# Output weights in runs of four rows, hidden units taken with a step of four, and two more loads of the second batch held behind a weight

## The chip, the cores and the metric

The kernel runs on one core of a Trainium2 chip. The metric is the device time of one execution in microseconds (us), lower is better. One execution was also taken by the hardware profiler; where a number below comes from its page or its trace, the time runs from the start of the profiled span.

## What is computed

The reference is an attention with 16 extra "beacon" keys, followed by a gated feed-forward network (FFN) over the same tokens:

```
B, H, S, Nb, D = 8, 8, 576, 16, 64
k_all = concat([beacon_k, k]);  v_all = concat([beacon_v, v])       # 592 keys for each head
scores = q @ k_all.T / 8, causal over the 576 own keys, beacons seen by all
a = softmax(scores);  x = a @ v_all                                  # 4608 tokens x 512
out = (relu(x @ w_gate) * (x @ w_val)) @ w_out                       # 512 -> 1536 -> 512
```

Inputs and output are float32 in memory. The order of the 1536 hidden units is free: any permutation gives the same output, if the columns of `w_gate` and `w_val` and the rows of `w_out` are permuted alike.

## The kernel before

Matrix work is done in bf16 with float32 sums. The kernel works batch by batch on the attention and span by span on the FFN: the spans are 240 and 336 tokens (together batch 0), then 512 each, and 448 at the end.

**Attention.** `new_batch` loads the inputs of a batch through staging tiles `st` (8 of them, `N_ST`): first two "rest" loads K and Q, then for each pair of heads a k load and a q load, and five v loads. The order of a batch after the first is the string `"KQ0011v2233vvvv"` (line 648), where 0 0 1 1 are k and q of head pairs 0 and 1, here called k0, q0, k1, q1 of batch 1. All these loads are issued by the SP engine, in one queue, in the planned order. GpSimd (POOL) or VectorE rounds a staged tile to bf16 (line 511, called the cast here), TensorE (PE) transposes it (line 522). Scores are line 740, the softmax is VectorE line 688, ScalarE line 695 and POOL line 706, the product with v is line 836.

**FFN.** `ffn(m0, mt, ...)` does, for each of 12 blocks of 128 hidden units, four matmuls on `wg_r` (line 897), ReLU on ScalarE (908), four matmuls on `wv_r` (902), the product on VectorE (913); then, for each 128 tokens, 12 matmuls on `wo_r` (928), an eviction to an `osb` tile (line 460 on ScalarE, 462 on VectorE) and a store (942). The weight operand of lines 897 and 902 (the part loaded into the array by LDWEIGHTS) is a contiguous slice of 128 columns. Only the very last piece of 64 tokens is done in two halves of 256 columns: both halves land in one `osb` tile, on partitions 0 to 63 and 64 to 127, the first half is stored by SP, the second by the queue of ScalarE.

**Weights.** Nine transfers, all issued by POOL (line 474), with a cast from float32 to bf16 on the way: gate and value in three column blocks each (512 columns, called g0, v0, g512, v512, g1024, v1024), and `w_out` in three blocks of four times 128 rows (wo0, wo4, wo8). Each of the nine consists of 512 runs of 512 values, 2 KB in memory and 1 KB in SBUF.

**The order of work** is written by a planner (`Plan.order`): every piece of work is a task with engines, a cost and a priority, and a list schedule with these costs fixes the order of the instructions of each engine. On the chip each engine goes through its own list in order, and waits only for data and buffers. A load can therefore be issued earlier than the planner thought, as soon as its staging tile is free. `HELD` is the means against it: `HELD[(b, at)]` gives the load at place `at` of batch `b` a marker on POOL (a memset of one element of its staging tile, line 532), which is planned behind the issue of the named weight; the load is behind the marker, and so are the batch's later loads. Before, only K of batch 1 is held, behind v0. While PE has nothing to do, the planner puts filler matmuls (line 987) into its list.

Of the kernel before, what the change touches and what calls it, by code (L numbers as in the profile page):

```python
# [34 lines left out]
PEQ = lambda b, g: b < 1  # L35
ENG = [("POOL", "DVE"), ("POOL",), ("POOL",)]
F_MOST = 3
HELD = {(1, 0): ("v", 0, 0)}
BEHIND = {(2, 7): (1, 1)}
MARK = 0.08  # L40
AB_FIRST = 0
# [4 lines left out]
OUT = -1300.0  # L46
ORDER0 = ("k00", "q00", "K", "Q", "k10", "q10", "v", "v", "k01", "q01", "k11", "q11", "v", "v", "v")
W_COLS = [(0, 512), (512, 512), (1024, 512)]
W_ROWS = 4
W0 = 9.0  # L50
W_STEP = 3.4
W_ISSUE = 0.85
# [114 lines left out]
class Plan:  # L167
# [7 lines left out]
    def add(self, engines, cost, run, deps=(), holds=(), prio=0.0, lag=None, part=0, lazy=0.0, after=0.0, move=0.0):  # L175
        t = Task(engines if isinstance(engines, tuple) else (engines,), cost, run, deps, holds, prio, lag, part, lazy, move)
        t.ready = after
        for d in t.deps:
            d.users.append(t)
        self.tasks.append(t)  # L180
        return t
# [108 lines left out]
def kernel(  # L290
# [12 lines left out]
    nc = tc.nc  # L303
# [5 lines left out]
    P = 128  # L309
# [29 lines left out]
    def many(n, shape, dtype, name):  # L339
        return [cp.tile(shape, dtype, name=f"{name}{i}") for i in range(n)]  # L340
# [4 lines left out]
    xT = cp.tile([P, KM, NT], BF16, name="xT")  # L345
    sel = xT[:, KM - 1, NT - 2 * P:].bitcast(FP32).rearrange("p (g j) -> p g j", j=TAIL)
    wg_r = cp.tile([P, KM, DFF], BF16, name="wg_r")
    wv_r = cp.tile([P, KM, DFF], BF16, name="wv_r")
# [14 lines left out]
    osb_s = Slots(many(N_OSB, [P, DM], FP32, "osb"))  # L363
# [10 lines left out]
    f_s, v_ps, first_ps = Share(banks, F_MOST), Share(banks, V_MOST), Share(banks, FIRST_MOST)  # L374
# [3 lines left out]
    add = plan.add  # L378


    def c_dve(n):
        return 0.07 + 0.00104 * n
# [7 lines left out]
    def c_act(n):  # L390
        return 0.06 + 0.00083 * n
# [4 lines left out]
    def c_pe(n):  # L396
        return 0.003 + n / 2400.0
# [60 lines left out]
    def copy(e, dst, src):  # L458
        if e == "ACT":
            nc.scalar.copy(dst, src)  # L460
        elif e == "DVE":
            nc.vector.tensor_copy(dst, src)  # L462
        else:
            nc.gpsimd.tensor_scalar(dst, src, 1.0, 1.0, ALU.mult, ALU.mult)  # L464
# [1 line left out]

    wg_s = moe_w_gate.rearrange("(ko ki) n -> ki ko n", ki=P)
    wv_s = moe_w_val.rearrange("(ko ki) n -> ki ko n", ki=P)
    wo_s = moe_w_out.rearrange("(ko ki) n -> ki ko n", ki=P)
    weight_in = {}  # L470

    def weight(kind, ko, kos, n0, w, prio, work):
        d, s = {"g": (wg_r, wg_s), "v": (wv_r, wv_s), "o": (wo_r, wo_s)}[kind]
        x = add("POOL", W_ISSUE, lambda t: nc.gpsimd.dma_start(
            d[:, ko:ko + kos, n0:n0 + w], s[:, ko:ko + kos, n0:n0 + w]), (), (), work, 0.1, move=0.78 * kos * w / 512,
            after=W0 + W_STEP * len(weight_in) / KM)
        for i in range(kos):
            for c in range(n0, n0 + w, 512):
                weight_in[kind, ko + i, c] = x
# [10 lines left out]
    def new_batch(b, prio, work):  # L490
# [35 lines left out]
        def staged():  # L526
            nonlocal held
            st = Hold(stage_s, 2)
            after = HELD.get((b, at)) or BEHIND.get((b, at))
            if after:  # L530
                st.users += 1
                held = add("POOL", MARK, lambda _: nc.gpsimd.memset(st.tile[:1, :1], 0.0), (), (st,), work - 30)
                if (b, at) in HELD:
                    weight_in[after].soon.append(held)
# [351 lines left out]
            one(what)  # L886


    def ffn(m0, mt, deps, prio):
        hid, vals = [], []  # L890
        hT = [Hold(hid_s, 1 + (mt + P - 1) // P) for _ in range(NF)]
        for nf in range(NF):
            psg, psv, g = Hold(f_s, 2), Hold(f_s, 2), Hold(gate_s, 2)

            def gate(_, nf=nf, psg=psg):
                for ki in range(KM):
                    nc.tensor.matmul(psg.tile[:, :mt], wg_r[:, ki, nf * P:(nf + 1) * P], xT[:, ki, m0:m0 + mt],  # L897
                                     start=(ki == 0), stop=(ki == KM - 1))

            def val(_, nf=nf, psv=psv):  # L900
                for ki in range(KM):
                    nc.tensor.matmul(psv.tile[:, :mt], wv_r[:, ki, nf * P:(nf + 1) * P], xT[:, ki, m0:m0 + mt],  # L902
                                     start=(ki == 0), stop=(ki == KM - 1))

            n0 = nf * P // 512 * 512
            a = add("PE", 4 * c_pe(mt), gate, deps + vals[max(nf - 3, 0):max(nf - 2, 0)] + [weight_in["g", ki, n0] for ki in range(KM)], (psg,),
                    prio + 0.02 * nf)
            r = add("ACT", c_act(mt), lambda _, psg=psg, g=g: nc.scalar.activation(  # L908
                g.tile[:, :mt], psg.tile[:, :mt], AF.Relu), (a,), (psg, g), -1000 + prio)
            b_ = add("PE", 4 * c_pe(mt), val, [a] + [weight_in["v", ki, n0] for ki in range(KM)], (psv,),  # L910
                     prio + 0.02 * nf + 0.01)
            vals.append(b_)
            hid.append(add("DVE", c_dve(mt), lambda _, psv=psv, g=g, nf=nf: nc.vector.tensor_mul(  # L913
                hT[nf].tile[:, :mt], g.tile[:, :mt], psv.tile[:, :mt]), (r, b_), (psv, g, hT[nf]), -1000 + prio))
        prev = None
        for t0 in range(0, mt, P):
            rows = min(P, mt - t0)

            halves = 2 if rows <= 64 else 1
            w = DM // halves  # L920
            ps, osb = Hold(f_s, 4 if halves == 1 else 3), Hold(osb_s, 2 * halves)
            prev = prev if halves > 1 else None
            k = NF // 3 * (2 * halves - 1)
            for part in range(NF // k):
                def outp(_, part=part, t0=t0, rows=rows, ps=ps, w=w, halves=halves, k=k):
                    for nf in range(k * part, k * part + k):
                        for c in range(halves):
                            nc.tensor.matmul(ps.tile[64 * c:64 * c + rows, :w], hT[nf].tile[:, t0:t0 + rows],  # L928
                                             wo_r[:, nf, w * c:w * c + w], start=(nf == 0), stop=(nf == NF - 1))

                need = [prev] + hid[k * part:k * part + k] + [weight_in["o", nf, 0] for nf in range(k * part, k * part + k)]
                if part == 0:
                    need += hid[:11]
                prev = add("PE", k * c_pe(w) + SWITCH * (halves - 1), outp, need, (ps,) + tuple(hT[k * part:k * part + k]),
                           prio + 0.3 + 0.01 * part - (0.5 if part else 0))
            for c in range(halves):
                def evict(x, c=c, ps=ps, osb=osb, rows=rows, w=w):
                    copy(x.engine, osb.tile[64 * c:64 * c + rows, :w], ps.tile[64 * c:64 * c + rows, :w])

                def store(_, c=c, osb=osb, rows=rows, t0=t0, w=w):  # L940
                    q_ = nc.scalar if c else nc.sync
                    q_.dma_start(out[m0 + t0:m0 + t0 + rows, w * c:w * c + w], osb.tile[64 * c:64 * c + rows, :w])

                ev = add("ACT" if c else ("ACT", "DVE"), {"ACT": c_act(w), "DVE": c_dve(w)}, evict, (prev,), (ps, osb), -1000 + prio)
                add("DMA", (0.4, 0.78 / halves), store, (ev,), (osb,), prio + OUT)


    T0 = 10.0
# [1 line left out]
    for n0, w in W_COLS:  # L950
        for kind in "gv":
            weight(kind, 0, KM, n0, w, -15 + 0.3 * i, WWORK + 0.01 * i - (50 if i < W_FIRST else 0))
            i += 1
    for ko in range(0, NF, W_ROWS):
        weight("o", ko, W_ROWS, 0, DM, -15 + 0.3 * i, WWORK + 0.01 * i - (50 if i < W_FIRST else 0))
        i += 1
# [20 lines left out]
    for i, (m0, mt) in enumerate(spans):  # L977
        deps = []
        for b in range(B):
            for what, lo, hi in (("AB", 0, G0), ("CDE", G0, G0 + G1), ("F", S - TAIL, S)):  # L980
                if b * S + lo < m0 + mt and b * S + hi > m0:
                    deps += [x_done[b, what, p] for p in range(NP if what != "F" else 1)]
        ffn(m0, mt, deps, 1000 + 10.0 * i)
# [37 lines left out]
```

## Time and profile before

| what | value |
|---|---|
| median of 3 runs | 407.6 us (406.13 to 408.1) |
| the profiled execution, whole | 406.64 us |
| its span on the core | 404.8 us |
| PE busy | 393.2 us, 97% |
| LDWEIGHTS busy | 206.6 us, 51% |
| VectorE, ScalarE, POOL busy | 293.5, 259.7, 233.4 us |
| TensorE clock granted | full (1.00) |
| DMA | 67.99 MB in 174147 packets, mean 168 GB/s |

The span is what lies between the first and the last instruction on the core; 1.84 us of the execution lie around it. A matmul's duration in the profile is longer than the distance to the next one, since matmuls are pipelined: a group of eight 512-column matmuls takes about 0.216 us for each further one. POOL issues the nine weight transfers at 15.7, 18.2, 23.0, 26.0, 29.8, 32.8, 45.2, 56.6 and 59.5 us. Queue q0 carries them, queue q1 all loads and stores of SP.

### The profile page before, as it was taken

How to read it: one execution, taken by the hardware profiler on the slowest of the kernel's cores; microseconds unless marked ns; L12 is line 12 of the kernel's file. 1: busy time of each engine (PE TensorE's matmuls, PEld its weight loads, DVE VectorE, ACT ScalarE, POOL GpSimd, SP SyncE). 2: the span in 40 equal slices, each digit the busy share in tenths (PEclk: the TensorE clock that was granted, in tenths of full speed). 3: DMA queues.
4: the chain of work that ended last, by engine and by line, in shares of the span. 5: the costliest groups of instructions: out<-in, count | busy, mean ns of one | idle time of the engine just before them, and what ended most of it. 6: DMA issues, size and time to landing. Idle time of an engine off the chain costs nothing.

```text
span 404.8 us, 9993 instructions
## 1 busy us (share of the span) xinstructions
PE 393.2 (97%) x3320; PEld 206.6 (51%) x3320; DVE 293.5 (73%) x1051; ACT 259.7 (64%) x809; POOL 233.4 (58%) x450
## 2 busy tenths in 40 slices
PE   7998999999999999999999999999999999999995
PEld 4666864655445545544454545454444454444543
DVE  4997799887877897777898988698777733442432
ACT  2988688857696896758695778588757721330320
POOL 6897769947495977576787778577564420000000
PEclk9999999999999999999999999999999999999999
DMA  7999897998998999979899999699848273001102
GB/s 182 216 222 214 182 219 143 198 181 235 191 230 185 238 181 255 197 175 192 227 194 203 249 233 176 164 306 212 154 78 175 42 145 125 0 0 53 52 2 91
DMA packets 174147, 67.99 MB, mean 168 GB/s; under 512 B 146384, under 2 KB 169552, under 8 KB 174096
## 3 DMA queue, kind: packets, MB, share of 16 engines
q1 hardware_dynamic: 169264, 62.57, 72.5%
q0 software_dynamic: 4752, 4.72, 7.3%
q8 instruction: 26, 0.43, 0.5%
q14 instruction: 25, 0.20, 0.2%
q10 hardware_dynamic: 80, 0.07, 0.1%
HBM read 38.54 MB, written 9.44 MB: 119 GB/s over the span
## 4 chain that ended last, share of the span: by engine, by line
PE 88%; POOL 5%; DMA 4%; DVE 1%; issue 1%; SPq 0%; ACT 0%; POOLq 0%
PE f L928 24%; PE f L902 23%; PE f L897 23%; PE f L740 7%; PE f L836 6%; PE f L522 4%; DMA wv_r<-in_moe_w_val_dram 3%; POOL xT L706 2%; PE f L859 1%; PE f L987 1%; POOL pb L706 1%; DMA st<-in_beacon_k_dram 1%; POOL v L464 1%; PE f L790 1%; DVE f L688 1%
## 5 line engine op out<-in xcount | busy, mean ns | idle before, releaser
L706 POOL TENSOR_SCALAR pb<-pb,small 128x320 bf16<-128x320 bf16 (+8 forms) x272 | 141.5, 538 | 80.7 <-DVE small L701 75.8
L695 ACT ACTIVATE pb<-f,small 128x320 bf16<-128x320 f32 (+8 forms) x272 | 144.5, 555 | 23.5 <-DVE small L688 14.0
L688 DVE CUSTOM_DVE_ANT_0 f<-f,mask 128x320 f32<-128x320 f32 (+8 forms) x288 | 134.3, 516 | 11.7 <-PE f L740 8.1
L897 PE MATMUL f<-xT,wg_r 128*128 128x512 bf16 (+3 forms) x480 | 106.2, 358 | 1.7 <-DMA wg_r<-in_moe_w_gate_dram 1.6
L902 PE MATMUL f<-xT,wv_r 128*128 128x512 bf16 (+3 forms) x480 | 107.0, 358 | 0.7 <-DMA wv_r<-in_moe_w_val_dram 0.7
L908 ACT ACTIVATE g<-f 128x512 f32<-128x512 f32 (+3 forms) x120 | 66.8, 567 | 62.3 <-PE f L897 58.1
L913 DVE TENSOR_TENSOR hT<-g,f 128x512 bf16<-128x512 f32 (+3 forms) x120 | 75.1, 632 | 38.5 <-PE f L902 35.1
L928 PE MATMUL f<-wo_r,hT 128*128 128x512 bf16 (+2 forms) x456 | 101.3, 374 | 0.0
L897 PEld LDWEIGHTS <-wg_r 128*128 128x128 bf16 x480 | 45.2, 98 | 45.0 <-DMA wg_r<-in_moe_w_gate_dram 1.8
L902 PEld LDWEIGHTS <-wv_r 128*128 128x128 bf16 x480 | 44.2, 98 | 43.4 <-issue 2.3
L928 PEld LDWEIGHTS <-hT 128*128 128x128 bf16 (+2 forms) x456 | 41.9, 100 | 47.6 <-issue 3.4
L695 ACT ACTIVATION_READ_ACCUMULATOR pb<-f,small 128x1 f32 x272 | 61.0, 224 | 0.0
L511 POOL TENSOR_SCALAR h<-st 128x512 bf16<-128x512 f32 (+1 forms) x92 | 48.4, 541 | 7.8 <-DMA st<-in_k_dram 2.2
L688 DVE DVE_READ_ACCUMULATOR2_ANT small<- 128x1 f32 x296 | 42.3, 143 | 0.2 <-issue 0.2
L740 PE MATMUL f<-kT,qT 64*64 64x64 bf16 (+7 forms) x640 | 35.5, 292 | 1.0 <-ACT pb L695 1.0
L462 DVE COPY osb<-f 128x512 f32<-128x512 f32 (+2 forms) x26 | 17.7, 681 | 23.8 <-PE f L928 23.7
L701 DVE RECIPROCAL small<-small 128x2 f32<-128x2 f32 (+3 forms) x144 | 22.1, 162 | 14.2 <-ACT pb L695 9.2
L522 PE MATMUL f<-ident,h 128*128 128x128 bf16 (+1 forms) x320 | 27.8, 219 | 1.1 <-POOL h L511 0.8
L522 PEld LDWEIGHTS <-h 128*128 128x128 bf16 (+1 forms) x320 | 20.9, 99 | 14.0 <-POOL h L511 3.5
L740 PEld LDWEIGHTS <-qT 64*64 64x64 bf16 x640 | 15.0, 105 | 23.8 <-issue 18.4
L836 PE MATMUL f<-pTb,v 128*64 128x320 bf16 (+3 forms) x488 | 26.0, 253 | 0.0
L836 PEld LDWEIGHTS <-v 128*64 128x64 bf16 (+1 forms) x512 | 20.6, 109 | 9.7 <-issue 7.2
(60 smaller groups left out, 235.3 us busy)
## 6 DMA issues: line engine op xcount, KB each, us to landing
out_dram<-osb SPq DMA_DIRECT2D x34, 256.0 KB, 2.3
st<-in_k_dram SPq DMA_DIRECT2D x32, 256.0 KB, 4.3
st<-in_q_dram SPq DMA_DIRECT2D x32, 256.0 KB, 4.8
st<-in_v_dram SPq DMA_DIRECT2D x24, 256.0 KB, 5.7
st<-in_v_dram SPq DMA_DIRECT2D x8, 224.0 KB, 5.3
wg_r<-in_moe_w_gate_dram POOLq DMA_DIRECT2D x3, 512.0 KB, 11.1
wv_r<-in_moe_w_val_dram POOLq DMA_DIRECT2D x3, 512.0 KB, 11.6
wo_r<-in_moe_w_out_dram POOLq DMA_DIRECT2D x3, 512.0 KB, 6.4
```

What stands on the lines that cost most here:

```text
L511: (nc.gpsimd if x.engine == "POOL" else nc.vector).tensor_scalar(to, src, by, 1.0, ALU.mult, ALU.mult)
L522: nc.tensor.matmul(to, h16.tile[:rows, a * P:(a + 1) * P], ident[:rows, :rows], start=True, stop=True)
L688: nc.vector.tensor_tensor_reduce(out=view(i, n - m), in0=view(i, n - m), in1=msk, scale=1.0, scalar=at(7) if m < n else 3.0e38, op0=ALU.ad ...
L695: nc.scalar.activation(ph.tile.rearrange("p a n -> p (a n)")[:, a:a + n], view(i), AF.Exp, bias=at(i), scale=-1.0, accum_out=at(4 + i))
L706: nc.gpsimd.tensor_scalar(one, one, at(8 + i), 1.0, ALU.mult, ALU.mult)
L740: nc.tensor.matmul(banks[k][b_].tile[64 * i:64 * i + 64, off:off + n], t.q.tile[r, 2 * g + i, 64 * j:64 * j + 64], t.kT.tile[r, 2 * g + i, ...
L836: nc.tensor.matmul(ps.tile[64 * hh:64 * hh + 64, d0:d0 + w], t.v.tile[:rows, c, D * h:D * h + D], rhs(64 * hh), start=(c == 0), stop=(c == ...
L897: nc.tensor.matmul(psg.tile[:, :mt], wg_r[:, ki, nf * P:(nf + 1) * P], xT[:, ki, m0:m0 + mt], start=(ki == 0), stop=(ki == KM - 1))
L902: nc.tensor.matmul(psv.tile[:, :mt], wv_r[:, ki, nf * P:(nf + 1) * P], xT[:, ki, m0:m0 + mt], start=(ki == 0), stop=(ki == KM - 1))
L908: r = add("ACT", c_act(mt), lambda _, psg=psg, g=g: nc.scalar.activation(g.tile[:, :mt], psg.tile[:, :mt], AF.Relu), (a,), (psg, g), -1000 ...
L913: hid.append(add("DVE", c_dve(mt), lambda _, psv=psv, g=g, nf=nf: nc.vector.tensor_mul(hT[nf].tile[:, :mt], g.tile[:, :mt], psv.tile[:, :m ...
L928: nc.tensor.matmul(ps.tile[64 * c:64 * c + rows, :w], hT[nf].tile[:, t0:t0 + rows], wo_r[:, nf, w * c:w * c + w], start=(nf == 0), stop=(n ...
```

## The change

Three things are changed together. `w_out` is read so that each partition gets four consecutive rows in one run of 8 KB; the hidden units of a block of 512 are thereby dealt out with a step of four, and the 128 columns that lines 897 and 902 take from `wg_r` and `wv_r` are every fourth one. Two more loads of batch 1 are held: k0 behind the issue of g1024, k1 behind the issue of v1024 (the loads between and after them follow in SP's queue). And each half of the last 64 tokens gets an `osb` tile of its own.

```diff
-HELD = {(1, 0): ("v", 0, 0)}
+HELD = {(1, 0): ("v", 0, 0), (1, 2): ("g", 0, 1024), (1, 4): ("v", 0, 1024)}
...
-    wo_s = moe_w_out.rearrange("(ko ki) n -> ki ko n", ki=P)
+    wo_s = moe_w_out.rearrange("(c ki ko) n -> ki c ko n", ki=P, ko=W_ROWS)
...
-        x = add("POOL", W_ISSUE, lambda t: nc.gpsimd.dma_start(
-            d[:, ko:ko + kos, n0:n0 + w], s[:, ko:ko + kos, n0:n0 + w]), (), (), work, 0.1, move=0.78 * kos * w / 512,
+        src = s[:, ko // W_ROWS] if kind == "o" else s[:, ko:ko + kos, n0:n0 + w]
+        x = add("POOL", W_ISSUE, lambda t: nc.gpsimd.dma_start(d[:, ko:ko + kos, n0:n0 + w], src), (), (), work, 0.1, move=0.78 * kos * w / 512,
...
+    def units(nf):
+        return nf // W_ROWS * W_ROWS * P + nf % W_ROWS
+
...
-                    nc.tensor.matmul(psg.tile[:, :mt], wg_r[:, ki, nf * P:(nf + 1) * P], xT[:, ki, m0:m0 + mt],
+                    nc.tensor.matmul(psg.tile[:, :mt], wg_r[:, ki, bass.ds(units(nf), P, step=W_ROWS)], xT[:, ki, m0:m0 + mt],
...
-                    nc.tensor.matmul(psv.tile[:, :mt], wv_r[:, ki, nf * P:(nf + 1) * P], xT[:, ki, m0:m0 + mt],
+                    nc.tensor.matmul(psv.tile[:, :mt], wv_r[:, ki, bass.ds(units(nf), P, step=W_ROWS)], xT[:, ki, m0:m0 + mt],
...
-            ps, osb = Hold(f_s, 4 if halves == 1 else 3), Hold(osb_s, 2 * halves)
+            ps, osb = Hold(f_s, 4 if halves == 1 else 3), [Hold(osb_s, 2) for _ in range(halves)]
...
-                def evict(x, c=c, ps=ps, osb=osb, rows=rows, w=w):
+                def evict(x, c=c, ps=ps, osb=osb[c], rows=rows, w=w):
...
-                def store(_, c=c, osb=osb, rows=rows, t0=t0, w=w):
+                def store(_, c=c, osb=osb[c], rows=rows, t0=t0, w=w):
...
-                ev = add("ACT" if c else ("ACT", "DVE"), {"ACT": c_act(w), "DVE": c_dve(w)}, evict, (prev,), (ps, osb), -1000 + prio)
-                add("DMA", (0.4, 0.78 / halves), store, (ev,), (osb,), prio + OUT)
+                ev = add("ACT" if c else ("ACT", "DVE"), {"ACT": c_act(w), "DVE": c_dve(w)}, evict, (prev,), (ps, osb[c]), -1000 + prio)
+                add("DMA", (0.4, 0.78 / halves), store, (ev,), (osb[c],), prio + OUT)
```

## The prediction

> **What bounds the kernel now.** I read the page's busy shares first: PE 97%, so the question is where PE has nothing useful to do. By the windows it is full (20.00 of 20) in every stretch from 100 to 360 us. What can be won lies ahead of that, and in the tail. The chain that ended last says how; this is its stretch from 29 to 47 us (start, length, what; the first line is its shares in that stretch):
>
> ```profile
> by line: DMA wv_r<-in_moe_w_val_dram 68.5%; POOL pb L706 7.9%; POOL wg_r L474 4.4%; POOL h L511 4.1%; PE f L902 3.2%; PE f L740 3.2%; PE f L816 2.5%; PE f L897 2.3%; PE f L836 2.2%; issue 1.7%; POOLq L511 0.2%
> ...
> 29.80 0.79 POOL wg_r L474
> ...
> 32.79 12.34 DMA wv_r<-in_moe_w_val_dram
> 45.13 0.05 issue
> 45.18 0.58 PE f L902 x4
> ```
>
> The last value block, v1024, is issued at 32.79 and lands 12.34 us later, at 45.13, and PE has waited for it. The timeline of PE shows the two waits for weights in that stretch, the bracket giving the idle time ahead:
>
> ```profile
> 34.23 0.58 PE L897 MATMUL f<-xT,wg_r 128*128 128x240 bf16 x4 [1.64 <-DMA wg_r<-in_moe_w_gate_dram]
> ...
> 45.18 0.58 PE L902 MATMUL f<-xT,wv_r 128*128 128x240 bf16 x4 [0.70 <-DMA wv_r<-in_moe_w_val_dram]
> ```
>
> So the wait that ends last is v1024's landing; from there the chain is PE, with a stretch on POOL from 55 to 62 us. Why 12.3 us for 512 KB? The DMA queues of three windows answer (28 to 32, 33 to 39, 48 to 50 us; queue: packets, MB, share of 16 engines):
>
> ```profile
> q0 software_dynamic: 489, 0.49, 73.1%
> q1 hardware_dynamic: 491, 0.48, 43.1%
> ```
>
> ```profile
> q0 software_dynamic: 934, 0.93, 91.0%
> q1 hardware_dynamic: 937, 0.25, 30.4%
> ```
>
> ```profile
> q0 software_dynamic: 366, 0.37, 116.8%
> q1 hardware_dynamic: 2, 0.00, 0.2%
> ```
>
> While both queues have work they take turns, packet by packet (489 to 491, 934 to 937). The weights' q0 then moves 122 packets a us beside 1-KB packets of the pair loads, 156 beside the 256-byte packets of v, and 183 alone. Each weight has 512. The Trainium skill's page "DMA: Bandwidth & Descriptors" (Queues, rings and completion order) says that an engine goes round robin over its queues at packet granularity; by these counts the trace agrees.
>
> **The change, part by part.**
>
> *The two holds.* Before, k0, q0, k1, q1 are issued at 22.43, 22.91, 23.54 and 24.00, while g512's packets begin at 27.5 (packet records), so the pairs run ahead of it and beside it. After: K of batch 1 shows what a marker does (memset at 19.50, 0.09 long, load issued at 19.61, though v0 landed only at 26.8): the hold ends with the weight's issue. So k0 goes at 29.80 + 0.79 + 0.09, about 30.8, q0 half a us later, k1 after v1024's issue (32.79 + 0.79) and one more POOL piece, about 34.5. A first packet comes 1.1 us after its issue (first load of the kernel: 0.81 to 1.94), so q0 has the engines alone from 27.5 to about 31.9. Counting packets of the four weights g512 to v1024 (4 x 512 = 2048):
>
> - before: 5.5 us at 122 (671 by 33.0), 6 us at 156 (1607 by 39.0), the last 441 beside k2 and q2 at 122: 42.6.
> - after: 4.4 us at 183 (805 by 31.9), then 1024 pair packets one to one at 122, 8.4 us (1829 by 40.3), the last 219 beside v at 156: 41.7.
>
> So v1024 comes 0.9 us earlier; the tail to the landing (42.6 to 45.13) is kept. g512 gains 1.4 (512/122 = 4.2 against 512/183 = 2.8), v512 1.6, g1024 0.7. The stall of 1.64 at 34.2 nearly goes; what is late next is v1024, for which PE then waits longer at line 902: in-order PE gives back what it won over 0.9. I book **-0.9** (bounds: 0, if g512's start slips; -2.3, both stalls).
>
> What is pushed back: the four pairs land at about 34 to 41 instead of 29.0, 31.0, 33.1, 35.4 (issue plus 6.6, 8.1, 9.6, 11.4). POOL casts them only here (engine, line, shapes):
>
> ```profile
> 44.63 0.62 POOL L511 TENSOR_SCALAR h<-st 128x512 bf16<-128x512 f32 x1
> ...
> 46.02 1.21 POOL L511 TENSOR_SCALAR h<-st 128x512 bf16<-128x512 f32 x2
> 48.35 0.62 POOL L511 TENSOR_SCALAR h<-st 128x512 bf16<-128x512 f32 x1 [1.12 <-issue]
> ```
>
> That slack hides the hold: k0 has 10 us, q1 some 7. SP's FIFO behind k0 holds only batch 1's own loads: v0 (landed 42.1, cast 48.93) comes about 1 us later, k2, q2, k3 wait for staging tiles until 32.15, 37.69, 41.09 anyway, and from 43.5 to 47 the DMA is nearly idle (q0 14, q1 315 packets) and takes what is late. No store or transpose of another batch is queued there yet. The markers put 2 x 0.09 on POOL at 30.7 and 34.4; v1024 queues behind g1024's packets, so its issue being 0.09 later costs nothing. If that cover were gone: 0.2.
>
> *Output weights in 8-KB runs.* A quarter of the runs, the same bytes. wo0 lands at 51.6 and is used at 55.0, wo4 at 63.0 and is used at 64.7 (planned fillers before it, no DMA wait), so faster landing is hidden by the order: nothing. The issue itself is on the chain twice, at 56.66 and 59.54, 0.73 and 0.74 long. The trace has no other count of runs on POOL; bounds 0 and -1.1 (three quarters of 1.47). The nearest rows are SP's issues: 0.37 us for a pair load of 256 runs, and also for a v load of 1024 at 46.67. Run count hardly shows, so I take **-0.1**.
>
> *Weights with a step of four.* 960 weight loads (480 + 480) read every fourth column. The trace has no stepped weight load. What it has (busy, mean ns; groups kept apart by shape, 60 to 95 us):
>
> ```profile
> L902 PEld LDWEIGHTS <-wv_r 128*128 128x128 bf16 x40 | 3.6, 98 | 1.9 <-issue 0.2
> ...
> L836 PEld LDWEIGHTS <-v 128*64 128x64 bf16 x56 | 2.1, 109 | 1.7 <-issue 1.5
> ...
> L928 PEld LDWEIGHTS <-hT 128*80 128x80 bf16 x12 | 1.3, 117 | 1.2 <-issue 0.2
> L928 PEld LDWEIGHTS <-hT 128*112 128x112 bf16 x8 | 0.9, 129 | 0.7 <-issue 0.2
> ```
>
> Loads of 64, 80 and 112 columns grow by about 0.42 ns a column; 128 columns break the line (98 instead of about 136): full loads have a faster form. Yet the slow 112-column load is hidden: four such matmuls take 1.07 us, (1.07 - 0.39)/3 = 0.227 apart against 0.217 for four with full loads (1.03), and one interruption is in it. The room is the distance of two matmuls: 0.102 us in the 240 span, 0.142, 0.189 and 0.216 in the others. A fast load needs at most 0.025 (line 859: twenty 32-column matmuls in 0.67 us, full loads), a slow 64-column one 0.041 (line 836, sixteen in 0.72), so a slow full one about 0.08, still under 0.102. So nothing, with both forms; nothing below nothing either, since a hidden load can't be hidden more. Upper bound below, as a rival. The Trainium skill's page "TensorE: Matmul & The Clock Gate" (Weight-path perf modes) speaks against the step: the fast load reads 32 bits at a time, two bf16, of which a step of four leaves one; it also says that the form is kept up to a step of 1,024. By it a load's reading would double, by the row above to 0.05, and the sum would stay the same; no stepped load is in this trace.
>
> *Two osb tiles.* The tail, on the chain:
>
> ```profile
> 400.60 0.42 DVE L462 COPY osb<-f 64x256 f32<-64x256 f32 x1 [0.74 <-PE f L928]
> 401.05 0.37 ACT L460 COPY osb<-f 64x256 f32<-64x256 f32 x1 [9.87 <-DVE osb L462]
> 401.44 0.56 ACTq L942 DMA_DIRECT2D out_dram<-osb  x1
> ```
>
> ScalarE waits for VectorE's write of the same tile. With its own it starts at 400.6, and the last store goes at 401.05, with SP's: **-0.4**. Its tile is free if the store of 398.15 has landed (2.0 us): it has. If not, the gain is 0.
>
> **The sum**: -0.9 - 0.1 - 0.4 = -1.4, from 406.64 (span 404.8 and 1.84 around it) to 405.2. The median of the runs shown lies 1.0 above the profiled one; carried over: **406.2** (own range 405.2 to 407.2).
>
> **Rivals.**
>
> 1. *Both stalls pay* (chance 0.28). The profile shows POOL and VectorE idle behind PE's 1.64 stall; if v1024's long tail shrinks too, 1.64 + 0.70 goes, and with the tail 0.4 and half of the wo bound 0.5 it is -3.2: 404.4. Against it: the packet count.
> 2. *Nothing moves but the tail* (0.10): g512's start at 27.5, 4.5 us after its issue, is not explained by the rows; if it waits for something that moves with the pairs, 407.2. That is also the case in which the holds don't do what they say.
> 3. *Head pairs late: slower* (0.13). The place is POOL's cast of q1 at 48.35; from there each us late is a us at the end, since PE has only that work next. It decides when q1 lands after 48. A marker that ended with the landing would do it: k1 issued at 45.2, q1 landing after 45.7 + 4.8 (median of q loads) = 50.5, +2.2 - 0.4: 409.4. K's marker speaks against it.
> 4. *A stepped load longer than a matmul: slower* (0.09). It decides from 0.102 us. At twice the slow form, 0.16, it costs 96 x 0.058 + 96 x 0.018 = 7.3 us in the first two spans and nothing later: 413.5. Above 0.216 all 960 pay, 1 us for each 1 ns. The hidden 112-column loads speak against it.
>
> The forecast has the other 0.40. A measurement here tells about 0.5% (2.0 us) from no change. Faster by more: all of rival 1, and a fifth of the forecast: 0.36. Slower by more: rivals 3 and 4 and a little noise: 0.25. Within: 0.39. The range reaches from the low side of rival 1 to rival 3: 403.8 to 409.4, leaving out rival 4 and the tails.
>
> **What would show it.** Right: k0 issued near 30.8, two more memsets on line 532; v1024's landing near 44.2; no stall at 34; casts of the pairs on POOL no later than 44.6 and 48.4; matmuls 0.216 apart; last ScalarE copy beside VectorE's. Wrong: PE waiting for line 522, or distances over 0.102 in the first span, or LDWEIGHTS well above 137 ns.

## The result and the profile after

The changed kernel takes **417.16 us** (median of 5 runs, 416.36 to 417.95) against 407.6 us for the kernel before (5 runs): ratio 1.0245, 95% interval 1.0218 to 1.0273. It is slower by about 10 us; the forecast was 406.2 and its range ended at 409.4. The profiled execution has a span of 415.0 us against 404.8. From here on the code has three more lines, so gate, value and output matmuls stand on lines 900, 905 and 931 (897, 902 and 928 before), the weights' issue on 475.

From the page: busy time of PE, and the rows of the granted clock and of the DMA over 40 slices of 10.4 us.

```profile
PE 395.8 (95%) x3276; PEld 222.7 (54%) x3320; DVE 293.7 (71%) x1051; ACT 260.4 (63%) x809; POOL 234.1 (56%) x452
...
PEclk9977899999999999999999999999999999999999
DMA  7994969799999799986999999899875455001102
```

The same two rows before:

```profile
PEclk9999999999999999999999999999999999999999
DMA  7999897998998999979899999699848273001102
```

Two marks are new in the first half: the clock falls to 0.7 in the third and fourth slice and 0.8 in the fifth (21 to 52 us), and the DMA is at 0.4 in the fourth. Both lie where the change works. The windows say it closer (window, length, busy time and count of PE, PEld, DVE, ACT and POOL; granted clock, DMA share, GB/s). Changed kernel:

```profile
30.00:35.00 5.00, 4.28 (x22) 2.60 (x23) 0.55 (x5) 3.05 (x10) 1.01 (x2) 0.50 0.71 107
35.00:40.00 5.00, 4.75 (x48) 3.68 (x47) 4.32 (x18) 2.89 (x9) 3.36 (x7) 0.88 0.15 8
40.00:45.00 5.00, 2.83 (x33) 2.22 (x32) 2.31 (x12) 2.51 (x8) 3.43 (x7) 0.81 1.14 239
```

Before:

```profile
30.00:35.00 5.00, 3.13 (x44) 2.67 (x42) 3.86 (x18) 3.03 (x8) 4.90 (x9) 1.00 1.20 226
35.00:40.00 5.00, 4.96 (x79) 3.60 (x78) 4.03 (x15) 4.88 (x15) 2.89 (x6) 1.00 1.21 200
```

PE looks busier than before from 30 to 35 us (4.28 against 3.13), but with half as many matmuls (22 against 44) at half the clock: busy time alone misleads here. And the DMA does nothing from 35 to 40 (8 GB/s), although five weights (g1024, v1024 and the three of `w_out`) and the pairs of batch 1 are still to come.

What PE waits for, in its timeline of the changed kernel (the bracket is the idle time ahead and what ended it):

```profile
28.28 0.39 PE L900 MATMUL f<-xT,wg_r 128*128 128x240 bf16 x1
30.73 0.79 PE L900 MATMUL f<-xT,wg_r 128*128 128x240 bf16 x3 [2.05 <-DMA wg_r<-in_moe_w_gate_dram]
...
40.84 0.26 PE L900 MATMUL f<-xT,wg_r 128*128 128x240 bf16 x1
43.27 0.79 PE L900 MATMUL f<-xT,wg_r 128*128 128x240 bf16 x3 [2.17 <-DMA wg_r<-in_moe_w_gate_dram]
```

The first two lines are hidden block 0, whose weights are in g0, on the chip since before 28 us: the first of its four matmuls runs, the second waits. The transfer that lands at 30.68 is g512, of which block 0 uses nothing. The other two lines are block 4, whose weights are in g512: its second matmul waits for g1024, which lands at 43.23. The chain that ended last goes through both:

```profile
24.83 5.85 DMA wg_r<-in_moe_w_gate_dram
30.68 0.05 issue
30.73 0.79 PE f L900 x3
...
37.67 5.56 DMA wg_r<-in_moe_w_gate_dram
43.23 0.05 issue
43.27 0.79 PE f L900 x3
```

And g1024 is issued only at 37.67, where it was 29.80. In POOL's timeline:

```profile
32.88 0.69 POOL L706 TENSOR_SCALAR pb<-pb,small 128x512 bf16<-128x512 bf16 x1 [2.57 <-DVE small L701]
35.92 1.15 POOL L706 TENSOR_SCALAR pb<-pb,small 128x320 bf16<-128x320 bf16 x2 [2.35 <-DVE small L701]
37.67 0.79 POOL L475 DMA_DIRECT2D wg_r<-in_moe_w_gate_dram  x1 [0.60 <-PE f L900]
```

POOL goes through its list in order. Ahead of the issue stand pieces of the softmax, which wait for VectorE. VectorE waits once (2.52 us) for ScalarE, whose ReLU of block 0 has waited 3.28 us for PE, and once (1.93 us) for scores that PE makes behind its own wait. The issue itself then waits another 0.60 us for gate matmuls.

### The profile page after: what moved, and what is told of

Read it like the earlier page. It is cut to its first block, busy times and chain, and to the rows that moved or that the text cites. A ratio compares the mean times of both kernels' runs of the same rounds, so it can differ in the third digit from the quotient of the medians.

```text
span 415.0 us, 9949 instructions
## 1 busy us (share of the span) xinstructions
PE 395.8 (95%) x3276; PEld 222.7 (54%) x3320; DVE 293.7 (71%) x1051; ACT 260.4 (63%) x809; POOL 234.1 (56%) x452
## 4 chain that ended last, share of the span: by engine, by line
PE 88%; DMA 8%; issue 1%; DVE 1%; POOL 1%; SPq 0%; ACT 0%; POOLq 0%
PE f L931 23%; PE f L900 23%; PE f L905 22%; PE f L740 6%; PE f L836 6%; PE f L522 4%; DMA wg_r<-in_moe_w_gate_dram 3%; DMA st<-in_v_dram 2%; DMA wo_r<-in_moe_w_out_dram 2%; PE f L859 1%; PE f L816 1%; PE f L990 1%; DMA st<-in_beacon_k_dram 1%; PE f L790 1%; DVE f L688 1%
## 5 line engine op out<-in xcount | busy, mean ns | idle before, releaser
L931 PE MATMUL f<-wo_r,hT 128*128 128x512 bf16 (+2 forms) x439 | 99.1, 374 | 1.8 <-issue 0.9
L900 PEld LDWEIGHTS <-wg_r 128*128 128x128 bf16 x480 | 52.7, 115 | 42.2 <-DMA wg_r<-in_moe_w_gate_dram 4.8
L905 PEld LDWEIGHTS <-wv_r 128*128 128x128 bf16 x480 | 51.6, 115 | 37.0 <-issue 2.4
L740 PE MATMUL f<-kT,qT 64*64 64x64 bf16 (+7 forms) x640 | 36.4, 295 | 2.2 <-ACT pb L695 1.4
L462 DVE COPY osb<-f 128x512 f32<-128x512 f32 (+2 forms) x26 | 17.7, 680 | 23.8 <-PE f L931 23.7
```

The costliest lines, as they stand in the source:

```text
L740: nc.tensor.matmul(banks[k][b_].tile[64 * i:64 * i + 64, off:off + n], t.q.tile[r, 2 * g + i, 64 * j:64 * j + 64], t.kT.tile[r, 2 * g + i, ...
L900: nc.tensor.matmul(psg.tile[:, :mt], wg_r[:, ki, bass.ds(units(nf), P, step=W_ROWS)], xT[:, ki, m0:m0 + mt], start=(ki == 0), stop=(ki == ...
L905: nc.tensor.matmul(psv.tile[:, :mt], wv_r[:, ki, bass.ds(units(nf), P, step=W_ROWS)], xT[:, ki, m0:m0 + mt], start=(ki == 0), stop=(ki == ...
```

## The theories

- **A.** The read with a step of four is tied to the transfers of the next column block. `wg_r` is one tile of 128 partitions by 4 rows by 1536. By address, the read of the second to fourth row of a block lies between the first and the last address of the next block's transfer, which covers columns of all four rows; a contiguous slice of 128 columns is seen to miss it, a stepped one is taken for an overlap. The first row's read lies ahead of that transfer's first address, which fits the one matmul that runs. So PE waits for data that it doesn't use. My first form of A had a second part: the next transfer in turn waits for matmuls that don't touch it (the 0.60 above), and the delay of the issue that comes of it is the larger loss.
- **B.** The stepped load itself is slow (rival 4 of the prediction).
- **C.** The holds are at fault: the pairs come too late (rival 3).

## The experiments

A ratio is always that to the kernel before on the same chip, whose median was 406.1 to 406.4 us in these runs.

**A tile for each column block.** `e1_split`: the changed kernel, with `wg_r` and `wv_r` as three tiles of 512 columns; loads, steps, holds and order stay.

```diff
-    wg_r = cp.tile([P, KM, DFF], BF16, name="wg_r")
+    wg_r = many(DFF // 512, [P, KM, 512], BF16, "wg_r")
...
-wg_r[:, ki, bass.ds(units(nf), P, step=W_ROWS)]
+wg_r[nf // W_ROWS][:, ki, bass.ds(nf % W_ROWS, P, step=W_ROWS)]
```

(and the same for `wv_r` and for the destinations of the transfers)

> The changed kernel with gate and value weights each in three SBUF tiles of 512 columns instead of one of 1536; the reads keep their step of four, the holds, the 8-KB runs and the two osb tiles stay. Theory A (each stepped read of one tile counts as touching everything between its first and its last column in all four row blocks, so it waits for the next column block, and the next block's transfer waits for the reads issued before it): both waits go, g1024 is issued near 30 us instead of 37.7, the first gate block runs at its own landing, and the time is 404 to 408 us. Rival B (the stepped weight load itself, 115 instead of 98 ns, costs the time): 415 to 418 us. Rival C (the holds cost it): 415 to 418 us too.

Measured: 404.95 us (404.42 to 406.64), ratio 0.9974 (0.9954 to 0.9994), span 403.1. PE's timeline:

```profile
24.83 0.60 PE L900 MATMUL f<-xT,wg_r 128*128 128x240 bf16 x4
...
32.66 0.57 PE L900 MATMUL f<-xT,wg_r 128*128 128x240 bf16 x4
```

Blocks 0 and 4 go through in one piece, no matmul waits for a weight, g1024 is issued at 30.05. The stepped loads are still there and still take 114 ns. B and C fall: the same steps and the same holds, without the tie, lose nothing against the kernel before.

**The old holds.** `e2_no_holds`: the changed kernel with `HELD` as before.

```diff
-HELD = {(1, 0): ("v", 0, 0), (1, 2): ("g", 0, 1024), (1, 4): ("v", 0, 1024)}
+HELD = {(1, 0): ("v", 0, 0)}
```

> The changed kernel without the two new holds. Theory A: the wait of g1024's issue for the gate matmuls stays, so 413 to 417 us, at most some 3 us better since the pairs of batch 1 are loaded early again. Rival C (the holds): 406 to 408 us. Rival B: 415 to 418 us.

Measured: 418.65 us (416.84 to 421.33), ratio 1.0307 (1.0262 to 1.0352), above what I had expected. The first wait is longer, since g512 shares the DMA with the pairs again and takes 9.8 us from issue to landing (23.43 to 33.25) instead of 5.85:

```profile
33.30 0.79 PE L900 MATMUL f<-xT,wg_r 128*128 128x240 bf16 x3 [7.95 <-DMA wg_r<-in_moe_w_gate_dram]
...
44.74 0.50 PE L900 MATMUL f<-xT,wg_r 128*128 128x240 bf16 x3 [2.25 <-DMA wg_r<-in_moe_w_gate_dram]
```

So without the holds the changed kernel is not faster; if anything they shield it a little (the two intervals just overlap). C falls again.

**The holds alone.** `e3_holds_only`: the kernel before with the new `HELD`.

> The kernel before with the two new holds alone (contiguous reads, 2-KB runs). The prediction's term: 0.9 us less than before, 406.2 to 407.2; k0 issued near 30.8 us, v1024 landing near 44.2. Rival C: 414 us or more. If the pairs are late on POOL: 408 to 410 us.

Measured: 405.0 us (404.04 to 408.28), ratio 0.9972 (0.9951 to 0.9993), or -1.1 us. k0 is issued at 32.08, k1 at 35.14, v1024 lands at 43.1 (issue at 33.48, 9.6 us), and neither of the two stalls for gate and value weights is left. A new one has come, for the output weights (it costs 0.38 us at each of the two places, from the start of the matmuls ahead to the start of these, against the kernel before):

```profile
63.01 1.02 PE L928 MATMUL f<-wo_r,hT 128*128 128x512 bf16 x4 [0.23 <-DMA wo_r<-in_moe_w_out_dram]
...
66.75 1.02 PE L928 MATMUL f<-wo_r,hT 128*128 128x512 bf16 x4 [0.22 <-DMA wo_r<-in_moe_w_out_dram]
```

**The step alone.** `e4_step_only`: the kernel before with the stepped reads of `wg_r` and `wv_r` and nothing else (the hidden units then come in another order than the rows of `w_out`).

> The kernel before with the stepped reads alone: old holds, 2-KB runs, so the hidden units of w_out no longer match those of gate and value. Theory A and rival B: 414 to 418 us; with A, g1024 is issued after 36 us and waits for line 897. Rival C: 407 to 408 us.

Measured: 418.36 us (417.12 to 418.9), ratio 1.029 (1.0267 to 1.0313); waits of 8.29 and 2.19 us on line 900. The second of them, and POOL's issue of g1024:

```profile
45.57 0.50 PE L900 MATMUL f<-xT,wg_r 128*128 128x240 bf16 x3 [2.19 <-DMA wg_r<-in_moe_w_gate_dram]
39.95 0.79 POOL L474 DMA_DIRECT2D wg_r<-in_moe_w_gate_dram  x1 [0.18 <-issue]
```

The step in the one tile is the whole loss. One thing did not come as expected: g1024 is late (39.95), but its issue waits for no matmul.

**Everything but the step.** `e5_contiguous`: the changed kernel with contiguous slices again. In its expectation and the next ones "the split kernel" or "the kernel with a tile for each column block" is `e1_split`, and C stands for the 8-KB runs.

> Everything of the changed kernel, but the gate and value weights are read as contiguous 128-column slices of the one tile again (the hidden units then don't match the rows of w_out). Theory A (the stepped read of the one tile is tied to the transfers of the next column block, and delays them): no wait of PE for weights from 20 to 60 us, g1024 issued near 30, 405 us like the kernel with a tile for each block, and LDWEIGHTS back at 98 ns where that one shows 115. If the 17 ns of a stepped load cost anything beside PE's matmuls, this one is faster than the split kernel by that: 1 us for each ns that isn't hidden. Theory C (the 8-KB runs of the output weights cost something): over 407.

Measured: 405.03 us (403.78 to 407.19), ratio 0.9959 (0.9931 to 0.9988): the same as the split kernel. g1024 is issued at 29.44, LDWEIGHTS is back at 98 ns.

**Which wait costs what.** `e6_first_apart` gives block column 0 a tile of its own and leaves the other two together; `e7_last_apart` leaves the first two together. Each keeps one of the two ties.

```diff
-    wg_r = cp.tile([P, KM, DFF], BF16, name="wg_r")
+    CUT = 1 * 512          # e7: 2 * 512
+    wg_r = [cp.tile([P, KM, w], BF16, name=f"wg_r{i}") for i, w in enumerate((CUT, DFF - CUT))]
```

(and the same for `wv_r`, the reads and the destinations of the transfers)

> The changed kernel with the first column block of each weight in a tile of its own and the other two together. Theory A: the first gate and value blocks no longer wait for g512 and v512, and g1024's issue no longer waits for PE (issued near 30); what is left is the wait of blocks 4 to 7 for g1024 and v1024, which come near 40 and 44: 407 to 411 us. If the whole loss were in that wait, 417.

> The changed kernel with the first two column blocks of each weight together and the last in a tile of its own. Theory A: the first gate block waits for g512 (some 2 us at 28), but g1024's issue waits for no matmul and blocks 4 to 7 wait for nothing of the last block: 406 to 409 us. If this one and the one with the first block apart lose far less than 12 us together, the larger part of the loss is the issue of g1024 that waited for PE's matmuls.

Measured: `e6` 410.38 us (409.4 to 412.75), ratio 1.0106 (1.007 to 1.0141); `e7` 413.12 us (412.62 to 413.59), ratio 1.0164 (1.0149 to 1.018), above what I had expected. PE in `e6`, where block 4 still waits for g1024:

```profile
32.89 0.26 PE L901 MATMUL f<-xT,wg_r 128*128 128x240 bf16 x1
35.85 0.50 PE L901 MATMUL f<-xT,wg_r 128*128 128x240 bf16 x3 [2.70 <-DMA wg_r<-in_moe_w_gate_dram]
```

A wait of 2.70 us, but the kernel loses 5.4 against the split one by the ratios (1.0106 - 0.9974 = 1.3%), 4.3 by the spans (407.4 - 403.1). The rest of the 4.3 is the clock. (The other three executions of `e6` have mean granted clocks of 0.989 to 0.994 against 0.996 in the profiled one, so they spent more time at half clock.) `e6` by windows of 1 us (length, PE busy and count, granted clock, DMA share, GB/s):

```profile
35.00:36.00 1.00, 0.15 (x2) 1.00 1.13 326
36.00:37.00 1.00, 1.00 (x11) 0.65 1.17 324
37.00:38.00 1.00, 1.00 (x10) 0.50 1.21 196
38.00:39.00 1.00, 1.00 (x14) 0.50 1.21 219
39.00:40.00 1.00, 1.00 (x11) 0.65 1.13 286
```

Just behind the wait PE runs at half clock for 3.4 us (0.7 + 1 + 1 + 0.7), which costs 0.35 + 0.5 + 0.5 + 0.35 = 1.7 us. 2.70 + 1.7 = 4.4, about the loss of the spans. The Trainium skill's page "TensorE: Matmul & The Clock Gate" (Part 1: The HAM clock gate) says that the clock is halved after an idle window of about 3.4 us and comes back after as long a busy one. The half agrees, and so do the 3.4 us in `e6`; other stretches at half clock last 6.8 us (`e7`, 28.5 to 35.3) and 10.2 us (the changed kernel, 26.0 to 36.2). The idle time does not agree: 2.70 us were enough here, and 2.17 in the changed kernel (half clock from 43.1 to 46.5 us). The 1.64 us of the kernel before left the clock at 1.00, but so did the 2.19 us of `e4` (1.00 in every window of 1 us from 43 to 49), and in `e2` the half clock came only 1.5 us behind the end of a wait of 2.25. The first stretch in the changed kernel even begins at 26.0, ahead of the wait for g512 and behind idle pieces of at most 1.16 us (PE busy 1.41 of 3 us from 23 to 26). So the length of one wait doesn't settle what the clock does. The stretches last once, twice or three times 3.4 us, as if the clock were decided only every 3.4 us; no run here tests that.

`e7`, where block 0 still waits for g512; PE, then POOL:

```profile
24.78 0.29 PE L901 MATMUL f<-xT,wg_r 128*128 128x240 bf16 x1
30.39 0.79 PE L901 MATMUL f<-xT,wg_r 128*128 128x240 bf16 x3 [5.32 <-DMA wg_r<-in_moe_w_gate_dram]
```

```profile
32.55 0.70 POOL L707 TENSOR_SCALAR pb<-pb,small 128x512 bf16<-128x512 bf16 x1 [4.20 <-DVE small L702]
35.59 1.07 POOL L707 TENSOR_SCALAR pb<-pb,small 128x320 bf16<-128x320 bf16 x2 [2.35 <-DVE small L702]
36.61 0.79 POOL L476 DMA_DIRECT2D wg_r<-in_moe_w_gate_dram  x1
```

The wait is 5.32 us, and the next gate block comes 7.55 us later than in the split kernel (36.18 against 28.63): 2.2 us are the half clock. More important is the last line. In `e7` nothing ties g1024's issue to a matmul, there is no wait in its bracket, and it is still at 36.61. So the second part of A falls as the larger loss: the issue is late because POOL's softmax pieces ahead of it are late. Of the 7.6 us by which the changed kernel issues g1024 later than the split one (37.67 against 30.05), the wait for matmuls is the last 0.60, and in `e2` and `e4`, with the same tie, there is no such wait. By the spans the two ties lose 407.4 - 403.1 = 4.3 and 410.6 - 403.1 = 7.5, together 11.8, and the changed kernel 415.0 - 403.1 = 11.9: they account for all of it, as far as one execution of each tells. (By the ratios it is 1.3% and 1.9%, or 13 us, against 11, with intervals of 0.2 to 0.4% on each.) That block 0 waits only 2.05 us in the changed kernel's profile, and not 5.32, is no gain: there it came 3.5 us later, behind a v load of 9.65 us (5.9 in `e7`; no run shows why), and g512 lands at about the same time in both, 30.68 and some 30.3.

**The stepped load by itself.** `e8_steps`: the split kernel, with 400 matmuls behind its end, in groups of 40, on a full weight load with steps of 1, 2, 4, 8 and 16.

```diff
+    for step in (1, 2, 4, 8, 16):
+        for n in (32, 128):
+            for _ in range(40):
+                nc.tensor.matmul(fill_bank[:, :n], flat[:, bass.ds(0, P, step=step)], xT[:, 0, :n], start=True, stop=True)
```

> The kernel with a tile for each column block, and behind its end 400 matmuls on a full weight load of 128 columns, with steps of 1, 2, 4, 8 and 16 and with 32 and 128 moving columns, 40 each. If a stepped load keeps the fast form at the same rate: 25 ns apart with 32 columns at every step. If its reading doubles: 50 ns at step 2 and over, and with 128 columns no change (about 55 to 60). If it falls into the slow form: some 80 ns with both.

Measured, the groups with 32 moving columns, one window for each step (length, busy and count of PE and PEld, clock):

```profile
399.70:400.72 1.02, 1.00 (x40) 1.01 (x41) 1.00 0.68 257
402.94:403.96 1.02, 1.02 (x44) 1.02 (x42) 1.00 0.07 16
406.18:407.48 1.30, 1.30 (x44) 1.30 (x41) 1.00 0.00 0
409.72:412.18 2.46, 2.46 (x44) 2.46 (x42) 1.00 0.00 0
414.63:417.05 2.42, 2.42 (x43) 2.42 (x42) 1.00 0.02 7
```

Forty matmuls in each: 25 ns apart at steps 1 and 2, 33 at step 4, 62 at 8 and 61 at 16. With 128 moving columns the distance is 56 ns up to step 4, and 61 and 63 at 8 and 16. So none of my three cases: step 2 is free, step 4 costs 8 ns, and from 8 on it is 2.5 times. The Trainium skill's page "SBUF — State Buffer" (Door 1: The DMA port swizzle) says that a step is free up to 8 bf16, by lines of 16 bytes in the memory; here a step of 4 already costs a third more where nothing hides it. In this kernel its 33 ns lie under matmuls of 102 to 216.

**What is left without the holds.** `e9_split_old_holds`: the split kernel with the old `HELD`.

> The kernel with a tile for each column block, with the old holds: what is left against the kernel before is the step, the 8-KB runs and the osb tiles. If the holds are worth the 1.1 us that they gave alone, and the other parts give nothing: 406.2, the same as before. If the 8-KB runs give something (POOL's issues of the output weights are 0.2 us shorter and two were on the chain): up to 0.5 under it. If the step costs anything beside the ties of the one tile: over 407.

Measured: 406.26 us (405.78 to 408.8), ratio 1.0006 (0.9991 to 1.0022). Step, 8-KB runs and osb tiles are together worth nothing; v1024's stall is back (0.58 at 45.63).

**The tail.** `e10_two_banks`: the split kernel, the last two halves summed in two PSUM tiles; `e11_banks_one_osb`: the same with one osb tile.

```diff
-            ps, osb = Hold(f_s, 4 if halves == 1 else 3), [Hold(osb_s, 2) for _ in range(halves)]
+            ps, osb = [Hold(f_s, 4 if halves == 1 else 3) for _ in range(halves)], [Hold(osb_s, 2) for _ in range(halves)]
```

(the matmuls and copies of a half then use `ps[c]`; `e11` has `[Hold(osb_s, 2 * halves)] * halves` for the osb tiles)

> The kernel with a tile for each column block, and the two halves of the last 64 tokens summed in two PSUM tiles instead of one. If ScalarE's last copy waits for VectorE because both read one PSUM tile: it now starts within 0.1 us of VectorE's, and the span ends 0.4 us earlier than that kernel's, 404.5. If something else ties it: ScalarE's copy still starts 0.45 us behind VectorE's, and 404.9.

> As the kernel with two PSUM tiles for the last halves, but with one osb tile for both again. If the osb tile ties the two copies as well (as the prediction took it): ScalarE's copy starts 0.45 us behind VectorE's. If only the PSUM tile does: within 0.1 us, and the two osb tiles of the change were needed for nothing.

The end of the changed kernel, with two osb tiles and one PSUM tile:

```profile
410.83 0.42 DVE L462 COPY osb<-f 64x256 f32<-64x256 f32 x1 [0.74 <-PE f L931]
411.28 0.37 ACT L460 COPY osb<-f 64x256 f32<-64x256 f32 x1 [9.87 <-DVE osb L462]
```

`e11`, with one osb tile and two PSUM tiles:

```profile
398.81 0.42 DVE L462 COPY osb<-f 64x256 f32<-64x256 f32 x1 [0.74 <-PE f L931]
398.85 0.37 ACT L460 COPY osb<-f 64x256 f32<-64x256 f32 x1 [9.44 <-PE f L931]
```

The releaser's name, "DVE osb L462", says only which instruction was waited for, not for which tile. It was the PSUM tile. In `e10` the copies are 0.03 us apart as well, and the span ends 3.9 us behind VectorE's copy (398.68 to 402.6) instead of 4.2 in the split kernel (398.88 to 403.1). In the time the 0.3 us don't show: 404.82 us (404.01 to 407.8), ratio 0.9972 (0.9956 to 0.9988); `e11` had 404.91 in one run.

## Where the time goes, load by load

All 3320 weight loads stand in the same order in these kernels (up to the end of the FFN), so the n-th of one can be set against the n-th of another. The table shows how many us later than before the n-th starts in the profiled executions:

| n (its time before) | holds alone (e3) | all but the step (e5) | split (e1) | changed |
|---|---|---|---|---|
| 300 (31.95) | 0.60 | -0.38 | 0.23 | 8.40 |
| 350 (37.15) | -1.12 | -2.11 | -1.49 | 10.38 |
| 450 (45.29) | -2.08 | -3.20 | -2.57 | 9.29 |
| 600 (58.25) | -2.08 | -3.20 | -2.57 | 9.29 |
| 700 (72.11) | -1.31 | -3.19 | -2.53 | 9.76 |
| 1800 (198.42) | -1.49 | -3.19 | -2.28 | 10.02 |
| 3319 (400.17) | -1.24 | -3.06 | -1.72 | 10.24 |

The changed kernel has lost everything by n = 350. The holds win 2.7 us between 32 and 45 us (0.60 to -2.08 in `e3`, 2.8 in `e1` and `e5`): 1.64 and 0.70 of it are the two stalls. In `e3` 0.8 of it is lost again between 58 and 72 us, where PE now waits for the output weights; in the two kernels with 8-KB runs it isn't. And from n = 600 on the kernels with stepped loads slip by 0.5 us or more (-2.57 to -1.72 with a step of 0.4 near 230 us; 0.47 in `e10`, 0.48 in `e9`, without that step), the contiguous one by 0.14. All of this is near or under what the runs' times can tell; the profiles alone show it, one execution each.

## Why the prediction was wrong, point by point

1. **What bounds the kernel now: right.** The stalls at 34 and 45 us were real and removable, and PE's order carried most of the gain to the end (-2.08 us at 45, -1.24 at 400 in `e3`).
2. **"The two holds", -0.9: the direction right, the number near by luck.** Alone they gave -1.1 us (by the interval -0.3 to -2.0). The holds do bring v1024 earlier, but the count of packets made too little of it: it lands at 43.1 in `e3` and 41.1 in `e1` (33.09 + 8.0), where I had 44.2. So PE did not give back at line 902 what it won at line 897. Both stalls went, and the movement on PE was -2.7, as in rival 1; 0.8 of it was lost again, which I did not foresee, and 0.6 only made good a later start of that execution. "What is late next" I had as v1024; it was the output weights. Rival 3 did not come: the pairs were in time wherever the tie was gone.
3. **"Output weights in 8-KB runs", -0.1: near.** The issue takes 0.59 us instead of 0.79, so run count does show on POOL, 0.2 for each. With the old holds they are worth nothing (`e9`). With the new ones they seem to save 0.8 us of waiting: "hidden by the order" held only for the order's timing before the holds. That is shown in profiles only.
4. **"Weights with a step of four": "So nothing, with both forms". This is the step that failed, by 11 us** (1.0245 - 0.9974). What it says of the load is right: the groups of the changed kernel from 60 to 95 us read

```profile
L905 PEld LDWEIGHTS <-wv_r 128*128 128x128 bf16 x56 | 5.8, 114 | 1.6 <-issue 0.2
L900 PEld LDWEIGHTS <-wg_r 128*128 128x128 bf16 x48 | 5.0, 114 | 1.8 <-issue 0.6
```

   114 instead of 98 ns, far from the 137 that I named as the mark of the slow form, and hidden up to some 0.5 us over the whole kernel. What failed is that I costed the instruction and left out its dependencies. A change of an operand's access pattern is also a change of what the instruction is taken to overlap, and so of what it waits for. I looked for a slower load (rival 4) and found a price on the right side, 413.5, by the wrong mechanism. The profile of before could have raised the question: PE uses the first 512 columns while the other 1024 of the same tile are still being written, so the order rests on slices being told apart. That, and not the load, was the thing to bound: block 0 waits for g512 and block 4 for g1024 (2.05 and 2.17 us in the changed kernel, 8.29 and 2.19 with the step alone), with the half clock beside these waits and a late issue of g1024, all on the path that sets the end.
5. **"Two osb tiles", -0.4: failed.** The wait stayed at 0.45 us because it belonged to the PSUM tile, as `e10` and `e11` show. I read the tile's name in the bracket as the reason.
6. **The sum.** With the tie gone the other parts together give -1.1 us (0.9974), where I had summed -1.4. But the holds alone give as much (`e3`), and the rest nothing (`e9`): the terms of -0.1 and -0.4 don't show in the time. What is left open: whether the 8-KB runs are worth their 0.8 us in the time, since the spread of the runs is as large, and how the overlap is worked out, which I infer from who waits (the first row of a block never, the others always) and from the split, and didn't see.

The versions `e3`, `e1`, `e5` and `e10` come out at about 405 us, 0.3 to 0.4% under the kernel before, with intervals that end just below 1; they are not to be told apart. Of those that compute the whole reference, the holds alone are the smallest edit.

## What to carry to other kernels

When an access pattern changes, ask what the instruction will be taken to overlap before asking how long it takes; where a tile is read while other parts of it are still being loaded, give each transfer a tile of its own. A wait's price on TensorE isn't always its length: in `e6` and `e7` the half clock behind it added 1.7 and 2.2 us, while a wait of 2.19 in `e4` brought none. And a releaser's name in a profile says who was waited for, not over which buffer.

## What the runs showed of the hardware

- Weight loads of 128 columns with 32-column matmuls: 25 ns apart at steps of 1 and 2, 33 at 4, 62 and 61 at 8 and 16.
- The granted clock fell to half in or up to 1.5 us behind idle times of TensorE of 2.17, 2.25, 2.70 and 5.32 us and stayed at 1.00 with 1.64 and, once, 2.19; the stretches at half clock lasted 3.4, 6.8 or 10.2 us.
- POOL's issue of a 512-KB weight takes 0.79 us as 512 runs of 2 KB and 0.59 as 128 of 8 KB.
